# A chunked RWKV-7 recurrence with a GELU layer: the loads of v, b and k issued behind N and its blocks, and the sums of decays in four 64x64 tiles

## Chip, cores and metric

The kernel runs on one core of one Trainium2 chip. The metric is the device time of one execution in microseconds (us). The core has a tensor engine (PE; its weight loads are listed as PEld), a vector engine (VectorE, DVE), a scalar engine (ScalarE, ACT), GpSimd (POOL) and SyncE (SP), which here issues nearly all transfers; sixteen DMA engines carry these out. All engines run in parallel, each through its own instructions in a fixed order, and wait for each other by semaphores.

## What is computed

The first block is a recurrence over 768 steps for 4 batches of 8 heads with 40 channels. The state is a 40x40 matrix for each head. The second block is a dense layer with exact GELU.

```python
for t in range(S):                      # S = 768; r, k, v, w, a, b: [4, 8, 768, 40]
    y[:, :, t] = einsum('bhd,bhde->bhe', rt, state)
    Sa = einsum('bhde,bhe->bhd', state, at)
    state = state * wt[:, :, None, :] - einsum('bhd,bhe->bhde', Sa, bt)
    state = state + einsum('bhd,bhe->bhde', vt, kt)
x = y.transpose(0, 2, 1, 3).reshape(3072, 320)
h = x @ w_in                            # 320 x 2048
out = (0.5 * h * (1 + erf(h / sqrt(2)))) @ w_out    # 2048 x 320
```

Everything is 32-bit floating point.

## The kernel before

**Chunks.** The 768 steps are cut into 12 chunks of 64 steps. Within a chunk the recurrence becomes matrix products: running products of the decay w (`sums`: logarithms times a triangle of ones, then Exp), scaled copies of a, b and k, the masked products N = b·a, A = k·a, RV = v·r and M, and the inverse of (1 - N). The state goes from one chunk to the next. On 128 partitions lie two halves of 64: `half(e)`. Four batches are two pairs: batch `G*e + g` has e = 0 or 1 for the half of the partitions and g = 0 or 1 for a place in a row.

**The loop of a chunk's inverse.** `make_N(c)` (L100 for the products, L549 for the mask on VectorE) writes N to DRAM with four transfers (L586). `start_inverse` reads the 32x32 diagonal blocks back as Nb (L635), one block to a partition, and GpSimd inverts them column by column: 31 columns, each a product (L643) and an addition (L645) in W. `store_inverse` writes W to DRAM as inv from GpSimd's own queue (L657). In the next iteration SyncE fetches it as Tt and T (L667, L671), VectorE turns a part of it to L (L680), and TensorE makes J from L and N (`corner`), X from the state (`make_X`), and so on.

**The main loop** runs over c from 2 to 11 and works on three chunks at once: the recurrence of chunk c, the products A, av and RV of chunk c + 1, and loads, decay sums, N and the inverse of chunk c + 2 (n and n2 in the code). Between these it calls `fill()`, which takes one piece of the dense layer of an earlier chunk: 40 matrix products of ph and a GELU (L901, L903), or, from the fourth chunk on, one of four steps of `seven`, a Strassen-like scheme for the second product with seven instead of eight block products (L854; its sums on VectorE are L858, L868, L869, L875). The order of every engine is the order of the program text: nothing is rescheduled.

**SyncE's order in an iteration** follows from that: four stores of results, w, a, r, b and v and k for the turned copies, the moves of the recurrence's output xt into the layout of the dense layer (L802, L805), then v into VR (L200), rows of b and of k (L153), then Tt and T of chunk n (L667, L671), then N of chunk n2 (L586) and Nb (L635). An issue whose operands aren't ready holds up all that follow. Transfers take one of eight semaphores in turn, and an issue waits, where needed, for the transfer that had the same one, eight before it.

**Names.** `w_tile` holds w and then its logarithm. `pt` (wT_ps in the profile) holds the running sums turned, 64 steps along the row; `wp` (wpT) and `en` are their Exp with plus and minus. `cum` holds the same sums with steps on partitions; their negative Exp `rw` (part) scales the rows of b (L463, VectorE, result `nb` in b_rows) and of k (L470, GpSimd, result `ks` in k_rows). Both are used late, in `make_QY`. `extra` and `NB = 4` belong to the first four chunks, which load and turn differently.

Of the kernel before, what the change touches and what calls it, by code (L numbers as in the profile page):

```python
# [12 lines left out]
ALU = mybir.AluOpType  # L13
# [6 lines left out]
def kernel(  # L20
# [78 lines left out]
    def mm(o, lhsT, rhs, first=True):  # L99
        nc.tensor.matmul(o, lhsT, rhs, start=first, stop=True, skip_group_check=True)  # L100
# [48 lines left out]
    def fetch(c, n, src, eng, t=None):  # L149
        if t is None:  # L150
            t = rows({"b": b_rows, "k": k_rows}[n][0 if c < NB else c % 2])
        for e in range(2):
            eng.dma_start(out=t[half(e)].rearrange("p g h d -> p (g h) d")[:, :, :D], in_=rows_of(src, c, e))  # L153
        raws[c, n] = t
# [23 lines left out]

    def load_w(c, t=None, eng=nc.sync):
        t = w_tile if t is None else t  # L180
        fetch(c, "w", w, eng, t[:, :G * DM].rearrange("p (g h d) -> p g h d", g=G, h=H))
        raws[c, "w"] = t

    def by_64(t):
# [8 lines left out]
    def load_kb(c):  # L193
        fetch(c, "b", b, nc.sync)
        fetch(c, "k", k, nc.sync)

    def load_VR(c):
        VR = turned_in.setdefault(c, {})["VR"] = VR_ring()
        for e in range(2):
            nc.sync.dma_start(out=VR[half(e)].rearrange("p g q m d -> p (g q m) d")[:, :, :D], in_=rows_of(v, c, e))  # L200
# [206 lines left out]
    def sums(c):  # L407
        logw = raws.pop((c, "w"))
        pt = duo("wT_ps").rearrange("p e (n t) -> p e n t", t=C)
        for n in range(G * NP):  # L410
            for x in range(2):
                for e in range(2):
                    at = (2 * n + x) * D
                    mm(pt[half(x), e, n], logw[half(e), at:at + HP], cum_m[half(e), half(e)])
        cum = duo("cum")[:, :, :DM]
        for g in range(G):
            mm(cum[:, g], cum_m, logw[:, g * DM:(g + 1) * DM])
        wp = wp_ring()
        nc.scalar.activation(wp[:, :, 1:].rearrange("p (n e) t -> p e n t", e=2), pt, ACT.Exp)
        turned_in.setdefault(c, {})["wp"] = wp  # L420
        if c >= NB:
            en = turned_in.setdefault(c, {})["en"] = by_batch(side("en", "kT", 1))
            nc.scalar.activation(en.rearrange("p (e n) t -> p e n t", e=2), pt, ACT.Exp, scale=-1.0)
        rw = (avs_ring if c in (1, 2) else part_ring)()[:, :, :DM]
        nc.scalar.activation(rw, cum, ACT.Exp, scale=-1.0)
        decays[c] = rw.rearrange("p g (h d) -> p g h d", h=H), wp
# [37 lines left out]
        turned_in[c]["nb"] = nb  # L464

    def scale_k(c, eng=nc.gpsimd):
        rwv, _ = decays.pop(c)
        ks = turned_in[c]["ks"] = padded[:, 2 + c % 2] if c < NB else k_rows[c % 2]
        to = ks[:, :, :, :D] if c < NB else rows(ks)
        eng.tensor_tensor(to, raws.pop((c, "k")), rwv, ALU.mult)  # L470
# [226 lines left out]
    def joined(c):  # L697
        t = turned_in[c]
        Tt, T2 = inverses.pop(c)
        Js = t.pop("Js")  # L700
        F = flat(Tt)
        J = duo("J2")[:, :, :G * NP * BL].rearrange("p z (n t) -> p z n t", n=G * NP)
        for n in range(2 * G * NP):
            for q in range(2):
                if n % 2:
                    mm(J[lo[q], 1, n // 2], Js[lo[q], n // 2], T2[lo[q], n // 2])
                else:
                    mm(J[lo[q], 0, n // 2], Js[hi[q], n // 2], F[hi[q], n, BL:])
        for q, copy in ((0, nc.scalar.copy), (1, nc.vector.tensor_copy)):
            copy(F[lo[q], :, BL:].rearrange("p (n z) t -> p z n t", z=2), J[lo[q]])  # L710
        t["Tt"] = Tt
# [115 lines left out]
    def block(g, z):  # L827
        return gt[:, z * NF // 2:(z + 1) * NF // 2, g * P:(g + 1) * P]
# [15 lines left out]
    def seven(c, s1, s2):  # L844
        t1, t2, t4 = sums_of_w
        t3 = quarter(0, 1)
        os = [work.tile([P, 2, DM // 2], FP32, tag="os", name="os", bufs=2) for g in range(G)]
        c11, c12, c21, c22 = os[0][:, 0], os[0][:, 1], os[1][:, 0], os[1][:, 1]

        def products_of(*factors):  # L850
            po = duo("po")
            for n, (l_, r_) in enumerate(factors):
                for f in range(NF // 2):
                    nc.tensor.matmul(po[:, n, :DM // 2], l_[:, f], r_[:, f], start=f == 0, stop=f == NF // 2 - 1)  # L854
            return po[:, 0, :DM // 2], po[:, 1, :DM // 2]

        def add(to, one_, other):
            nc.vector.tensor_tensor(to, one_, other, ALU.add)  # L858

        def store(g):  # L860
            for e in range(2):
                row = (G * e + g) * S + c * C
                nc.sync.dma_start(out=out[row:row + C], in_=os[g][half(e)].rearrange("p z d -> p (z d)"))

        m1, m2 = products_of((block(0, 0), quarter(0, 0)), (block(0, 1), quarter(1, 0)))
        if s2 is None:
            s2 = SM_ring().rearrange("p e g n c -> p (e g n c)")[:, :NF * P // 2].rearrange("p (f t) -> p f t", t=P)
            nc.vector.tensor_tensor(s2, s1, block(0, 0), ALU.subtract)  # L868
        nc.vector.tensor_tensor(block(1, 0), block(0, 0), block(1, 0), ALU.subtract)  # L869
        nc.scalar.copy(c12, m1)  # L870
        nc.scalar.copy(c11, m2)
        add(c11, c11, c12)
        yield
        m5, m6 = products_of((s1, t1), (s2, t2))
        nc.vector.tensor_tensor(block(0, 1), block(0, 1), s2, ALU.subtract)  # L875
        nc.scalar.copy(c22, m5)  # L876
        add(c12, c12, m6)
        yield
        m3, m7 = products_of((block(0, 1), quarter(1, 1)), (block(1, 0), t3))
        add(c21, c12, m7)  # L880
        add(c12, c12, c22)
        add(c12, c12, m3)
        add(c22, c22, c21)
        store(0)
        yield
        m4, _ = products_of((block(1, 1), t4))
        add(c21, c21, m4)
        store(1)
        yield
# [231 lines left out]
    for c in range(2, NCH):  # L1121
        n, n2 = c + 1, c + 2
        more, more2 = n < NCH, n2 < NCH
        corner(c)
        make_X(c)
        if c == NS + 1:
            weight_sums(3)
        if c == 2:

            seconds(1, (14, 14), last=True)  # L1130
            fill()
            turn_b(n)
            make_N(n)
            run(start_inverse(n, nc.gpsimd))
            store_inverse(n, (nc.gpsimd,))
            load_r(n)
            load_v(n)
        else:
            fill()
        if more2:  # L1140
            load_next(n2)
        joined(c)
        if c == 2:
            pieces.reverse()
            seconds(2, last=True)
        fill()
        make_sa(c)
        make_saT(c)
        if c == 2:
            turn_r(n)  # L1150
            scale_k(n, nc.vector)
            fill()
            pieces.reverse()
            fill(2)
            turn_k(n)
        if more2:
            load_r(n2)
        if more2:
            turn_a(n2)
            fetch_pairs(n2, "b_turned", b, nc.sync, False, paired["a"])  # L1160
        fill()
        make_y2(c)
        make_M(c)
        if more:
            turn_v(n)
        if more2:
            load_v(n2)
            turn_r(n2)
            fetch_pairs(n2, "k_turned", k, nc.sync, False, paired["r"])
        fill()  # L1170
        if more2:
            logs(n2)
        make_QY(c)
        outputs(c)
        pieces.append(mlp(c))
        fill()
        if c == NS:
            weight_sums(0)
            weight_sums(1)
        if more:  # L1180
            make_A(n)
        if more2:
            load_VR(n2)
            load_kb(n2)
            sums(n2)
        if more:
            turn_state()
            fetch_inverse(n)
            make_av(n)
        if more2:  # L1190
            scale_a(n2)
            turn_b(n2)
        fill()
        if c == NS:
            weight_sums(2)
        if more:
            make_RV(n)
        if more2:
            make_N(n2)
            scale(n2)  # L1200
            run(start_inverse(n2, nc.gpsimd))
            store_inverse(n2, (nc.gpsimd,))
        if more:
            turn_corner(n)
        fill()
        if more2:
            turn_k(n2)
        fill()
# [31 lines left out]
```

## Time and profile before

| What | Value |
|---|---|
| Time, median of 3 runs (lowest, highest) | 731.21 us (728.41, 731.35) |
| Span of the profiled execution | 724.5 us |
| PE busy | 663.1 us (92%) |
| PEld busy | 582.5 us (80%) |
| DVE busy | 383.5 us (53%) |
| POOL busy | 352.8 us (49%) |
| ACT busy | 213.8 us (30%) |
| Mean rate of all transfers | 105 GB/s, 75.75 MB in all |
| GpSimd waits for Nb (10 times) | 104.9 us |
| GpSimd waits for k before L470 (8 times) | 64.9 us |
| SyncE waits for inv before Tt (4 times) | 23.7 us |

The table gives busy time and waits over the whole run. A long wait of an engine tells only that it has nothing to do; whether it costs anything depends on who waits for that engine next. So three views matter more here: the chain of waits that ended last, the timeline of each engine around one chunk, and busy time in stretches from one X to the next. In a timeline row the columns are the start, the length, the engine, the line, the operation and tiles, the count, and in brackets the idle time before it with what ended it.

### The profile page before, as it was taken

What the parts mean: (1) busy time and instruction counts of PE and PEld (TensorE: products, weight loads), DVE (VectorE), ACT (ScalarE), POOL (GpSimd) and SP (SyncE); (2) the same over time, 40 slices, a digit from 0 to 9 for tenths busy, and PEclk for the clock granted to TensorE, in tenths of its full rate; (3) what the DMA queues carried; (4) which work ended last, traced back from release to release, by engine and by line L of the source; (5) the groups of instructions that cost most, each with busy time, mean ns of one, the idle gap of its engine ahead of it and who ended that gap; (6) DMA issues with size and microseconds to landing.
All of it is one profiled execution on the core that took longest, in us unless ns stands there. A gap on an engine that the chain in (4) does not pass through costs nothing.

```text
span 724.5 us, 31335 instructions
## 1 busy us (share of the span) xinstructions
PE 663.1 (92%) x14096; PEld 582.5 (80%) x14096; DVE 383.5 (53%) x541; ACT 213.8 (30%) x279; POOL 352.8 (49%) x794
## 2 busy tenths in 40 slices
PE   6455889569999999999999999999999999999997
PEld 4345778557787887899899898998898998888987
DVE  2786569885255176275374473663762752621403
ACT  5114455343141240341341332222312413112020
POOL 4285248810761671862852853863854845810000
PEclk9655799779999999999999999999999999999999
DMA  7887739653766747657666666656566561020000
GB/s 118 135 168 145 138 93 216 132 109 80 132 129 99 144 85 137 108 99 137 109 115 126 113 113 125 116 95 132 111 102 125 104 106 50 22 53 3 25 14 19
DMA packets 284302, 75.75 MB, mean 105 GB/s; under 512 B 271976, under 2 KB 276872, under 8 KB 284168
## 3 DMA queue, kind: packets, MB, share of 16 engines
q1 hardware_dynamic: 283104, 71.22, 52.0%
q0 software_dynamic: 864, 2.36, 1.8%
q8 instruction: 111, 1.82, 1.1%
q14 instruction: 23, 0.19, 0.1%
q10 hardware_dynamic: 200, 0.16, 0.1%
HBM read 59.54 MB, written 10.22 MB: 96 GB/s over the span
## 4 chain that ended last, share of the span: by engine, by line
PE 49%; POOL 19%; DMA 10%; SPq 7%; DVE 7%; issue 5%; ACT 2%; ACTq 1%; DVEq 0%; POOLq 0%
PE ph L901 17%; POOL W L645 8%; POOL tmp L643 8%; PE po L918 8%; PE po L854 7%; PE QY L100 3%; DMA inv<-W 3%; DMA N<-N 3%; DMA Nb<-N 2%; PE cum L100 1%; PE J L100 1%; POOL st L643 1%; SPq L153 1%; POOL st L645 1%; PE X L100 1%
## 5 line engine op out<-in xcount | busy, mean ns | idle before, releaser
L901 PE MATMUL ph<-xt,w_in_sb 64*128 64x256 f32 x1920 | 221.1, 383 | 0.8 <-ACT gt L903 0.8
L901 PEld LDWEIGHTS ph<-xt,w_in_sb 64*128 64x128 f32 x1920 | 183.4, 188 | 23.9 <-ACT gt L903 0.5
L643 POOL TENSOR_TENSOR tmp<-W,Nb 128x126 f32<-128x126 f32 (+22 forms) x310 | 129.7, 418 | 128.4 <-DMA Nb<-N 104.9
L645 POOL TENSOR_TENSOR W<-W,tmp 128x126 f32<-128x126 f32 (+22 forms) x310 | 133.7, 431 | 24.3
L903 ACT ACTIVATE gt<-ph 128x1024 f32<-128x1024 f32 x48 | 49.1, 1023 | 148.6 <-PE ph L901 124.5
L854 PE MATMUL po<-w_out_sb,gt 128*128 128x160 f32 x576 | 82.9, 302 | 0.1
L854 PEld LDWEIGHTS po<-w_out_sb,gt 128*128 128x128 f32 x576 | 78.7, 190 | 2.2 <-DVE gt L875 0.4
L918 PE MATMUL po<-w_out_sb,gt 128*128 128x320 f32 x192 | 55.3, 444 | 0.0
L918 PEld LDWEIGHTS po<-w_out_sb,gt 128*128 128x128 f32 x192 | 36.6, 194 | 15.4 <-issue 1.1
L470 POOL TENSOR_TENSOR k_rows<-k_rows,part 128x640 f32<-128x640 f32 x8 | 12.3, 1542 | 64.9 <-DMA k_rows<-in_k_dram 64.9
L549 DVE TENSOR_TENSOR SM<-M_ps,upper 128x1024 f32<-128x1024 f32 x12 | 14.7, 1224 | 46.1 <-PE M_ps L100 46.1
L710 DVE COPY Tt<-J 32x512 f32<-32x512 f32 x12 | 8.3, 689 | 54.0 <-ACT Tt L710 54.0
L694 ACT COPY Js<-J 128x256 f32<-128x256 f32 x12 | 4.5, 371 | 101.6 <-PE J L100 101.6
L906 DVE TENSOR_TENSOR half<-gt 128x1024 f32<-128x1024 f32 x9 | 11.8, 1308 | 38.6 <-ACT gt L903 38.6
L303 ACT ACTIVATE conv<-conv,rebias 128x320 uint32<-128x320 uint32 (+1 forms) x26 | 16.1, 625 | 35.4 <-DVE conv L302 35.1
L854 PE MATMUL po<-extra,half 128*128 128x160 f32 x176 | 26.1, 303 | 0.0
L738 DVE COPY SM<-sap 128x640 f32<-128x640 f32 x12 | 9.9, 824 | 28.3 <-PE sap L100 28.2
L903 ACT ACT_TABLE_LOAD x10 | 12.8, 1283 | 40.0 <-PE ph L901 39.9
L854 PEld LDWEIGHTS po<-extra,half 128*128 128x128 f32 x176 | 24.2, 190 | 0.3
L858 DVE TENSOR_TENSOR os<-os,po 128x160 f32<-128x160 f32 x36 | 11.3, 315 | 24.8 <-ACT os L876 14.5
L549 DVE TENSOR_TENSOR VR<-RV_ps,upper 128x1024 f32<-128x1024 f32 x12 | 14.7, 1224 | 17.3 <-PE RV_ps L100 17.3
L680 DVE STREAM_TRANSPOSE L<-Tt 128x512 f32<-128x512 f32 x12 | 8.5, 711 | 27.4 <-DMA Tt<-inv 27.4
(197 smaller groups left out, 1130.6 us busy)
## 6 DMA issues: line engine op xcount, KB each, us to landing
Nb<-N SPq DMA_DIRECT2D x22, 256.0 KB
VR<-in_v_dram SPq DMA_DIRECT2D x24, 160.0 KB
out_dram<-os SPq DMA_DIRECT2D x48, 80.0 KB
w_tile<-in_w_dram SPq DMA_DIRECT2D x22, 160.0 KB
b_rows<-in_b_dram SPq DMA_DIRECT2D x22, 160.0 KB
k_rows<-in_k_dram SPq DMA_DIRECT2D x22, 160.0 KB
w_out_sb<-in_moe_w_out_dram SPq DMA_DIRECT2D x11, 320.0 KB
N<-N SPq DMA_DIRECT2D x48, 64.0 KB
```

The source lines that it names most:

```text
L100: nc.tensor.matmul(o, lhsT, rhs, start=first, stop=True, skip_group_check=True)
L303: nc.scalar.activation(power, power, ACT.Relu, bias=rebias, scale=8.0)
L470: eng.tensor_tensor(to, raws.pop((c, "k")), rwv, ALU.mult)
L549: nc.vector.tensor_tensor(to, pt, upper.unsqueeze(1).to_broadcast([P, 2 * G * NP, C]), ALU.mult)
L643: eng.tensor_tensor(t, W[:, :rows, j:j + 1].to_broadcast([P, rows, rest]), Nb[:, j:j + 1, j + 1:].to_broadcast([P, rows, rest]), ALU.mult)
L645: eng.tensor_tensor(W[:, :rows, j + 1:], W[:, :rows, j + 1:], t, ALU.add)
L854: nc.tensor.matmul(po[:, n, :DM // 2], l_[:, f], r_[:, f], start=f == 0, stop=f == NF // 2 - 1)
L858: nc.vector.tensor_tensor(to, one_, other, ALU.add)
L901: nc.tensor.matmul(ph[:, x, s], w_in_sb[half(x), kt, p * P:(p + 1) * P], xt[half(x), kt], start=kt == 0, stop=kt == NK - 1)
L903: nc.scalar.activation(gt[:, 4 * q:4 * q + 4].rearrange("p (x s) t -> p x s t", x=2), ph, ACT.Gelu)
L906: nc.vector.tensor_tensor(s1, block(1, 0), block(1, 1), ALU.add)
L918: nc.tensor.matmul(po[:, g], gt[:, f, g * P:(g + 1) * P], w_out_sb[:, f], start=f == 0, stop=f == NF - 1)
```

## The change

It has five parts, all for the chunks that the main loop prepares.

- The loads of b and k rows and of v (VR) move from ahead of Tt, T, N and Nb to behind them in SyncE's order, so that N and its blocks needn't wait for them.
- GpSimd's scaling of k moves from ahead of the inverse to after its eighth column (`BL // 4`), since k now comes later. `decays` keeps its entry, so that b can be scaled after k.
- VectorE's scaling of b moves into the next iteration, after `joined`.
- In `seven`, the subtraction that makes block(1,0) moves behind that of block(0,1).
- From the fifth chunk (`c >= NB`) w's pair g = 1 is loaded with its two batches in exchanged halves. Then the four sums of cum (two halves, two pairs) are four 64x64 products, one in each quadrant of the array, in place of two products of 128x128 with a triangle whose off-diagonal quarters are zero. As the turned sums come out with e exchanged for g = 1, the two Exps that read them are split into two each, with the order put right as they write.

```diff
     def load_w(c, t=None, eng=nc.sync):
         t = w_tile if t is None else t
-        fetch(c, "w", w, eng, t[:, :G * DM].rearrange("p (g h d) -> p g h d", g=G, h=H))
+        to = t[:, :G * DM].rearrange("p (g h d) -> p g h d", g=G, h=H)
+        if c < NB:
+            fetch(c, "w", w, eng, to)
+        else:
+            for e in range(2):
+                for g in range(G):
+                    eng.dma_start(out=to[half(e ^ g), g],
+                                  in_=w[G * e + g, :, c * C:(c + 1) * C].rearrange("h t d -> t h d"))
...
         for g in range(G):
-            mm(cum[:, g], cum_m, logw[:, g * DM:(g + 1) * DM])
+            for e in range(1 if c < NB else 2):
+                q = half(e ^ g) if c >= NB else slice(0, P)
+                mm(cum[half(e) if c >= NB else q, g], cum_m[q, q], logw[q, g * DM:(g + 1) * DM])
         wp = wp_ring()
-        nc.scalar.activation(wp[:, :, 1:].rearrange("p (n e) t -> p e n t", e=2), pt, ACT.Exp)
         turned_in.setdefault(c, {})["wp"] = wp
-        if c >= NB:
+        if c < NB:
+            nc.scalar.activation(wp[:, :, 1:].rearrange("p (n e) t -> p e n t", e=2), pt, ACT.Exp)
+        else:
             en = turned_in.setdefault(c, {})["en"] = by_batch(side("en", "kT", 1))
-            nc.scalar.activation(en.rearrange("p (e n) t -> p e n t", e=2), pt, ACT.Exp, scale=-1.0)
+            for to, scale_ in ((wp[:, :, 1:].rearrange("p (g n e) t -> p g e n t", g=G, e=2), 1.0),
+                               (en.rearrange("p (e g n) t -> p g e n t", e=2, g=G), -1.0)):
+                for g in range(G):
+                    nc.scalar.activation(to[:, g], pt[:, ::1 - 2 * g, g * NP:(g + 1) * NP], ACT.Exp, scale=scale_)
...
     def scale_k(c, eng=nc.gpsimd):
-        rwv, _ = decays.pop(c)
+        rwv, _ = decays[c]
...
-        nc.vector.tensor_tensor(block(1, 0), block(0, 0), block(1, 0), ALU.subtract)
         nc.scalar.copy(c12, m1)
         nc.scalar.copy(c11, m2)
         add(c11, c11, c12)
         yield
         m5, m6 = products_of((s1, t1), (s2, t2))
         nc.vector.tensor_tensor(block(0, 1), block(0, 1), s2, ALU.subtract)
+        nc.vector.tensor_tensor(block(1, 0), block(0, 0), block(1, 0), ALU.subtract)
...
         joined(c)
+        if c > 2 and more:
+            scale_b(n)
...
         if more2:
-            load_VR(n2)
-            load_kb(n2)
             sums(n2)
...
             make_N(n2)
-            scale(n2)
-            run(start_inverse(n2, nc.gpsimd))
+            steps = start_inverse(n2, nc.gpsimd)
+            load_kb(n2)
+            load_VR(n2)
+            for _ in range(BL // 4):
+                next(steps)
+            scale_k(n2)
+            run(steps)
             store_inverse(n2, (nc.gpsimd,))
```

## The prediction

> **What bounds the kernel now.** I read the page's chain of waits first. Its shares name two bounds, TensorE and a loop of GpSimd and DMA:
>
> ```profile
> PE 49%; POOL 19%; DMA 10%; SPq 7%; DVE 7%; issue 5%; ACT 2%; ACTq 1%; DVEq 0%; POOLq 0%
> ```
>
> The chain in order of time separates them. From 252 to 415 us it is TensorE alone. From 415 to 645 us it is one round repeated: N to DRAM, its blocks back (Nb), the inverse on GpSimd, the inverse to DRAM (inv), Tt back. Next, busy time chunk by chunk (stretch, length, then PE, PEld, DVE, ACT, POOL, granted clock, DMA share, GB/s):
>
> ```profile
> 338.20:388.90 50.70, 50.70 (x1184) 46.16 (x1180) 28.24 (x35) 15.41 (x20) 29.29 (x68) 1.00 0.65 117
> 439.70:491.30 51.60, 50.76 (x1182) 46.17 (x1182) 28.57 (x35) 15.40 (x20) 31.73 (x68) 1.00 0.60 114
> 491.30:543.10 51.80, 50.81 (x1184) 46.15 (x1180) 28.56 (x35) 15.41 (x20) 31.85 (x68) 1.00 0.62 116
> 543.10:596.50 53.40, 52.49 (x1190) 47.43 (x1182) 28.42 (x35) 15.41 (x20) 32.07 (x68) 0.97 0.60 112
> ```
>
> The first row has no idle TensorE: 50.7 us is its own price of a chunk. In the others it waits about 0.9 us each (the last also has a clock of 0.97). TensorE's timeline says for what:
>
> ```profile
> 489.51 0.74 PE L100 MATMUL J<-L,N 32*32 32x32 f32 x64 [0.84 <-DVE L L680]
> 541.37 0.74 PE L100 MATMUL J<-L,N 32*32 32x32 f32 x64 [0.98 <-DVE L L680]
> 594.75 0.74 PE L100 MATMUL J<-L,N 32*32 32x32 f32 x64 [0.91 <-DVE L L680]
> ```
>
> L is turned from Tt, so these are waits for the loop. Chunk 11 adds 0.65 us at J, chunk 10 0.96 at av. Together 4.3 us: all that a quicker loop alone can give. More must come out of the 50.7 us.
>
> SyncE's timeline shows why the loop is late (start, length, transfer):
>
> ```profile
> 424.98 1.41 SPq L200 DMA_DIRECT2D VR<-in_v_dram  x2
> 426.45 2.12 SPq L153 DMA_DIRECT2D b_rows<-in_b_dram  x2
> 428.61 3.58 SPq L153 DMA_DIRECT2D k_rows<-in_k_dram  x2
> 432.62 3.18 SPq L667 DMA_DIRECT2D Tt<-inv  x4
> 435.85 0.99 SPq L671 DMA_DIRECT2D T<-inv  x2
> 436.94 2.02 SPq L586 DMA_DIRECT2D N<-N  x4
> ```
>
> VectorE had N masked at 432.7, yet N is issued at 436.9, behind the rows. In the five rounds from 225 us on, issue minus mask is 4.5, 2.3, 1.8, 2.5 and 4.2 us. After that SyncE waits for inv itself, and the loop runs on its own length: 51.8 us from Tt at 486.20 to Tt at 537.98.
>
> **What the skill says.** The Trainium skill, SBUF — State Buffer, "Who interferes with whom": a DVE instruction with two SBUF inputs contends with a GpSimd instruction that reads SBUF, and the later one blocks. The trace agrees: the inverse's 56-element add takes 0.30 us at 502.36, but 1.22 at 528.69, inside nT times en on VectorE (528.52 to 529.75). The skill's TensorEngine Tiling, "Tiling Modes": 64x64 gives four independent tiles. It agrees: one 64x104 matmul instruction of QY lasts 249 ns, 128 of them take 3.01 us, 23.5 ns each. The skill's DMA: Bandwidth & Descriptors, "Queues, rings and completion order": a ring's descriptors are consumed in order, so rows behind Nb should not overtake it; the trace of before has no such order to show it.
>
> **The change, part by part.**
>
> *Rows of v, b, k behind N and Nb.* Their six issues take 5.1 us (476.39 to 482.31) to 7.2 us. In the SyncE-bound rounds N now goes when masked, 1.8 to 4.5 us earlier. In the round after 415 us: mask at 432.7 less 2.8 (the tiles below, five chunks) is 429.9; Tt and T in front of N cost 3.05 us after inv has landed (486.20 to 489.24), which gives about 431 instead of 436.9, a lead of 6 us. Further, inv travels without the rows: with rows beside it 6.3, 5.0 and 6.4 us from issue to Tt, without them (635.59 to 640.78) 5.2; I take 5.2, a gain of about 0.7 a round.
>
> *k scaled after eight columns.* The 1.54 us of L470 used to lie in GpSimd's wait for Nb (11.0 us at 499.99) and cost nothing. Now it lies inside the inverse: +1.54 us a round. Should k be late, GpSimd waits with 23 columns queued behind: k's issue ends about 4 us after Nb's, rows land some 4 us after that (482.31 to 486.62), and Nb plus eight columns needs 5 + 6 us (499.99 to 506.1). It arrives first, by about 3 us: no wait.
>
> *b scaled after joined.* 0.82 us on VectorE, put before SM, where it waits 2.76 us for sap: hidden for TensorE. But it has two SBUF inputs and now falls in the inverse: 0 to 0.8 us, I take 0.5.
>
> *block(1,0) later.* 1.42 us on VectorE (521.76) leaves the stretch ahead of A's mask and runs after L875, ahead of the second half of a product pair whose first half takes 2.3 us of TensorE: hidden. If the inverse has ended by then (4 us of lead suffice), one block of GpSimd, about 0.9 us, goes.
>
> *Four 64x64 tiles for cum.* Before: four instructions of 128x320, 1.18 us from cum's start to the next (319.93 to 321.11). Four tiles need eight instructions of about 0.27 us; side by side as QY's are (3.7 times) 0.58 us plus a start, so 0.63; one after another more than 1.18. I take the first: 0.55 us saved in each of eight chunks, 4.4 us, on the path wherever TensorE is the bound. It is the only edit that lowers the 50.7.
>
> *Exps in halves.* wp and en, 1.03 and 1.02 us, become four of 512 elements; that size costs 0.59 alone and starts every 0.49 in a pair (saT at 503.24 and 503.72). +0.1 us on ScalarE before en is done; po takes that buffer about 0.5 us later. No cost. w's four issues for two: at most 0.5 us of SyncE.
>
> *What the rows delay.* Out, w and a now queue behind six issues. Also the program lets each issue wait for the DMA eight before it, which today holds a back until Nb has landed (issue at 500.19, Nb at 499.99); after, out waits so. I put a 7 us later. VectorE turns a at 506.42, 16.2 us after X; 7 us later it would push M's mask, which QY awaits at X + 24.0, by 1.6 us. This bites only where X follows Tt's issue by 4.1 us, as now; with 6 us or more between them it vanishes. It limits itself, so I cost it at 0.5 us in all.
>
> **The sum.** A round is 3.05 (Tt, T) + 10.1 (N issue to first column, 489.24 or 384.51 on) + inverse + 5.2. The inverse took 30.2 to 31.3 us while X came 6 to 10 us after Tt's issue, and 33 when it came 4 us after, since then more of VectorE's two-input work falls into it. With the lead restored: 31.3 + 1.54 + 0.5 - 0.9 = 32.4, and the round is 50.8 against TensorE's new 50.15. From N at 431 three rounds and the last inverse end at 431 + 3 x 50.8 + 10.1 + 32.4 + 5.2 = 631.1. The last X needs that plus 4.1, 635.2; TensorE alone brings it to 644.9 - 4.3 - 4.4 = 636.2. So the loop is just hidden: 8.7 us, less 0.5, leaves 731.2 - 8.2 = 723 us.
>
> **Rivals.** *The loop still binds the end.* For: the reserve is 1 us over four rounds, and scaled k is pure addition. With a round of 52.3 the last inverse lands at 637.2 and X at 641.3: 3.6 us gained, 728. *The tiles don't run side by side:* only the waits go, 4.3 us, 727. Against: QY's 23.5 ns. *The loop gets longer than it was.* Rows behind Nb slow it by 0.7, the inverse stays at 33 and pays 1.54 + 0.8: 54.4 a round, last inverse at 645.4, X at 649.5, 4.6 us later than now: 736. For: the blocks seen on GpSimd and the late a, which keeps VectorE's work inside the inverse. Against: inv's freer path, and a lead of 6 us at the start.
>
> **Chances.** Forecast 723: 0.53, with some of it down to 719, where the rounds shrink and nothing else is lost. Loop still binds, 728: 0.22. Tiles serial, 727: 0.10. Longer loop, 736: 0.15. The bound of 0.5% is 3.7 us, 727.5: faster gets 0.53, half of the two middle cases (0.16), 0.69 in all; same 0.16; slower 0.15. The range for eight in ten: 718 to 732.
>
> **What would show it.** Right: cum at about 0.6 us a chunk; N issued within 0.5 us of its mask until about 430 us; J waits gone or under 0.3 us; PE's rows at 50.1 without idle; the inverse about 32.5 us with k's scaling inside and no wait before it. Wrong: waits at J as now; GpSimd idle before k's scaling; the inverse at 35 us; VectorE waiting for a and TensorE for M's mask at QY; SyncE reaching Tt after inv has landed.

## The result and the profile after

| | Median, us | Ratio to before (95% interval) |
|---|---|---|
| Before, 4 runs | 730.09 | |
| Changed kernel, 4 runs | 718.38 | 0.9853 (0.9807 to 0.9900) |
| Changed kernel again, 22 runs, beside 55 of before (median 730.16) | 723.41 | 0.9895 (0.9866 to 0.9925) |

The change is a gain. Its size is better read from the second row: 1.05%, or 7.7 us. Medians are over all runs; the ratios leave out runs more than 1.5% above the fastest of their kernel, among them the one that was profiled in the second measurement. For the second measurement 721 to 723 us were expected from the two profiles, and 718 to 719 if the first measurement's 11.7 us were all the change's; 723.4 came.

Times scatter by some 10 us from run to run. Part of this lies at the start: the third X, which ends the part with the weight conversions, starts at 232 to 234 us in some profiles and at 237 to 240 in others. The granted clock differs there: 0.86 between 60 and 120 us in the changed kernel's profile (third X at 232.5), 0.79 in that of e6 (238.0). So kernels are compared below by time and by the stretch from the third X to the last. This stretch fell from 411.4 us (233.5 to 644.9) to 403.4 (232.5 to 635.9), 8.0 us.

The stretch scatters too. The second measurement's profile of the changed kernel, e5, is of an execution of 728.6 us. Its stretch is 407.4 us (239.4 to 646.8), only 4.0 us shorter than before's, and its last J waits long for the loop:

```profile
646.10 0.74 PE L100 MATMUL J<-L,N 32*32 32x32 f32 x64 [2.07 <-DVE L L693]
```

TensorE is idle for 5.1 us of the stretch, against 2.0 in the first profile; its busy time is nearly the same, 402.3 and 401.4 us, and its clock 1.00 in both. A difference of up to 4 us between the stretches of two kernels therefore proves little by itself. What follows in this section is from the first profile.

In the chain, GpSimd's share falls from 19% to 16%, and the others move by at most a point. Busy time chunk by chunk in the changed kernel (columns as before: length, then PE, PEld, DVE, ACT, POOL, clock, DMA share, GB/s):

```profile
335.50:385.60 50.10, 50.10 (x1190) 45.51 (x1184) 29.20 (x35) 15.53 (x22) 29.00 (x68) 1.00 0.64 114
385.60:435.70 50.10, 50.10 (x1194) 45.52 (x1184) 28.52 (x35) 15.53 (x22) 28.80 (x68) 1.00 0.65 119
435.70:486.60 50.90, 50.42 (x1196) 45.68 (x1184) 28.43 (x35) 15.53 (x22) 28.97 (x68) 1.00 0.66 119
486.60:537.10 50.50, 50.35 (x1187) 45.61 (x1184) 28.68 (x35) 15.53 (x22) 29.88 (x68) 1.00 0.64 117
```

TensorE's price of a chunk is now 50.1 us. Idle time is left in two of these rows (0.5 and 0.15 us). SyncE's timeline of the round that was shown for before:

```profile
426.74 2.10 SPq L680 DMA_DIRECT2D Tt<-inv  x4
428.88 1.96 SPq L684 DMA_DIRECT2D T<-inv  x2
430.94 2.04 SPq L599 DMA_DIRECT2D N<-N  x4
434.50 1.14 SPq L648 DMA_DIRECT2D Nb<-N  x2
435.73 1.37 SPq L153 DMA_DIRECT2D b_rows<-in_b_dram  x2
437.15 3.61 SPq L153 DMA_DIRECT2D k_rows<-in_k_dram  x2
440.80 1.57 SPq L207 DMA_DIRECT2D VR<-in_v_dram  x2
```

N goes at 430.9 where it went at 436.9, with the mask done at 429.9. In the four rounds before this one it goes within 0.1 us of its mask. TensorE's timeline around cum (tn_ps, the turned state, comes next), before and then after:

```profile
318.87 1.13 PE L100 MATMUL wT_ps<-cum_m,w_tile 64*64 64x64 f32 x64
319.93 1.34 PE L100 MATMUL cum<-w_tile,cum_m 128*128 128x320 f32 x4
321.11 1.04 PE L433 MATMUL tn_ps<-ident,st 128*128 128x128 f32 x8
```

```profile
317.84 1.11 PE L100 MATMUL wT_ps<-cum_m,w_tile 64*64 64x64 f32 x64
318.77 0.72 PE L100 MATMUL cum<-w_tile,cum_m 64*64 64x320 f32 x8
319.42 1.09 PE L446 MATMUL tn_ps<-ident,st 128*128 128x128 f32 x8
```

From the same engine's timeline, its waits in the first two rounds and the last (av is the product of VR and A):

```profile
215.42 1.14 PE L100 MATMUL av<-VR,A 64*64 64x40 f32 x64 [0.61 <-ACT en L436]
268.26 1.14 PE L100 MATMUL av<-VR,A 64*64 64x40 f32 x64 [0.45 <-ACT en L436]
621.23 1.14 PE L100 MATMUL av<-VR,A 64*64 64x40 f32 x64 [0.32 <-DVE A L562]
635.26 0.74 PE L100 MATMUL J<-L,N 32*32 32x32 f32 x64 [0.54 <-DVE L L693]
```

From wT_ps to tn_ps takes 1.58 us where it took 2.24. The wait for en is new, and the wait of the last J is what remains of the four.

In the whole stretch TensorE's idle time fell from 4.3 to 2.0 us and its busy time from 407.0 to 401.4. Of the 5.6 us of busy time 1.7 are before's chunk with a clock of 0.97, in which TensorE ran at half clock for some 3.4 us, right behind the wait of 0.98 us at J (541.37):

```profile
544.00:546.00 2.00, 2.00 (x14) 1.60 (x12) 1.77 (x3) 0.00 (x0) 0.00 (x0) 0.50 0.10 12
```

Other profiles have such stretches too; the last section counts them. The other 3.9 us are TensorE's lower price of a chunk, over seven chunks.

### The profile page after: what moved, and what is told of

The parts are those of the page before. It is cut to its first block, busy times and chain, and to the rows that moved or that the text cites. A ratio compares the mean times of both kernels' runs of the same rounds, so it can differ in the third digit from the quotient of the medians.

```text
span 716.1 us, 31454 instructions
## 1 busy us (share of the span) xinstructions
PE 656.9 (92%) x14128; PEld 575.5 (80%) x14128; DVE 383.7 (54%) x541; ACT 214.6 (30%) x295; POOL 343.6 (48%) x794
## 4 chain that ended last, share of the span: by engine, by line
PE 49%; POOL 16%; DMA 11%; DVE 8%; SPq 7%; issue 5%; ACT 3%; ACTq 1%; POOLq 0%; DVEq 0%
PE ph L914 18%; PE po L931 8%; POOL W L658 8%; PE po L867 8%; POOL tmp L656 7%; PE QY L100 3%; DMA inv<-W 3%; DMA Nb<-N 2%; DMA N<-N 2%; PE J L100 2%; SPq L153 1%; DMA Tt<-inv 1%; DMA w_out_sb<-in_moe_w_in_dram 1%; DVE conv L314 1%; PE av L100 1%
## 5 line engine op out<-in xcount | busy, mean ns | idle before, releaser
L656 POOL TENSOR_TENSOR tmp<-W,Nb 128x126 f32<-128x126 f32 (+22 forms) x310 | 125.0, 403 | 164.4 <-DMA Nb<-N 141.5
L658 POOL TENSOR_TENSOR W<-W,tmp 128x126 f32<-128x126 f32 (+22 forms) x310 | 129.4, 418 | 24.3
L176 DVE STREAM_TRANSPOSE aT<-a_pairs 128x1024 f32<-128x1024 f32 x9 | 11.2, 1245 | 43.2 <-DMA a_pairs<-in_a_dram 43.2
L100 PE MATMUL av<-VR,A 64*64 64x40 f32 x768 | 15.7, 240 | 9.0 <-DVE A L562 7.3
L100 PEld LDWEIGHTS av<-VR,A 64*64 64x64 f32 x768 | 14.0, 149 | 11.3 <-DVE A L562 7.9
```

The source lines that it names most:

```text
L176: nc.vector.transpose(to.rearrange("p n (s y) -> p n y s", y=2), raws.pop((c, n)).rearrange("p n (y d) -> p n y d", y=2)[:, :, :, :BL])
L656: eng.tensor_tensor(t, W[:, :rows, j:j + 1].to_broadcast([P, rows, rest]), Nb[:, j:j + 1, j + 1:].to_broadcast([P, rows, rest]), ALU.mult)
L658: eng.tensor_tensor(W[:, :rows, j + 1:], W[:, :rows, j + 1:], t, ALU.add)
```

## The experiments

Each has a share of the change undone or done alone. In the table, the inverse is the mean time of the last four from their first column to the issue of inv. The first profile of the changed kernel stands for it; in its second, e5, the stretch is 407.4 us and the inverse 33.1.

| Kernel | Median, us | Ratio (95% interval) | Third X to last, us | Inverse, us |
|---|---|---|---|---|
| before | 730.16 | | 411.4 | 32.6 |
| changed | 723.41 | 0.9895 (0.9866 to 0.9925) | 403.4 | 32.6 |
| e1: tiles alone | 729.82 | 0.9995 (0.9968 to 1.0021) | 413.5 | 31.8 |
| e11: tiles, block | 725.41 | 0.9943 (0.9915 to 0.9971) | 409.6 | 31.6 |
| e2: rows alone | 725.95 | 0.9934 (0.9911 to 0.9957) | 406.9 | 33.3 |
| e10: rows, block | 722.31 | 0.9896 (0.9850 to 0.9943) | 406.4 | 32.0 |
| e3, e7: rows, tiles | 726.66, 725.76 | 0.9952, 0.9956 | 407.1, 407.9 | 33.8, 33.7 |
| e4, e6: changed, k on VectorE | 723.09, 722.57 | 0.9872, 0.9892 | 403.9, 402.8 | 31.4, 31.2 |
| e9: as e6, block first | 722.44 | 0.9893 (0.9840 to 0.9947) | 403.7 | 32.3 |
| e12: as e6, no tiles | 724.12 | 0.9926 (0.9900 to 0.9953) | 406.1 | 30.6 |
| e8: rows between T and N | 773.78 | 1.0579 (1.0509 to 1.0648) | 448.4 | 34.0 |

("Rows" includes k after eight columns and b after joined; "block" is block(1,0)'s move.)

**e1: tiles alone.** The kernel before with `load_w` and `sums` of the change, nothing else.

```diff
-            mm(cum[:, g], cum_m, logw[:, g * DM:(g + 1) * DM])
+            for e in range(1 if c < NB else 2):
+                q = half(e ^ g) if c >= NB else slice(0, P)
+                mm(cum[half(e) if c >= NB else q, g], cum_m[q, q], logw[q, g * DM:(g + 1) * DM])
```

> The kernel before with one part of the change: w's exchanged halves, cum in four 64x64 tiles, Exps in halves. Theory (two bounds that need each other): TensorE's price of a chunk falls by 0.6 us, from 50.7 to 50.1, but the rows still stand ahead of N, so the loop of GpSimd and DMA keeps its length of about 52 us and binds earlier. Expected: waits at J of 1.2 to 1.8 us in the last three or four rounds where there were 0.9, and a gain of only 2 to 3 us of the 4.8 that the tiles are worth; span 721.5 to 722.5. Rival (the loop was never the bound, its waits were slack): the full 4.8 us, span below 720.

No gain at all: 0.9995. TensorE's timeline still has the waits at J, one of them at 1.53 us:

```profile
391.62 0.74 PE L100 MATMUL J<-L,N 32*32 32x32 f32 x64 [0.91 <-DVE L L693]
497.83 0.74 PE L100 MATMUL J<-L,N 32*32 32x32 f32 x64 [1.53 <-DVE L L693]
```

The first comes two chunks earlier than any such wait did before. And SyncE still holds N: its mask was done at 440.7.

```profile
435.10 2.10 SPq L207 DMA_DIRECT2D VR<-in_v_dram  x2
437.25 1.69 SPq L153 DMA_DIRECT2D b_rows<-in_b_dram  x2
438.98 3.07 SPq L153 DMA_DIRECT2D k_rows<-in_k_dram  x2
442.16 2.25 SPq L680 DMA_DIRECT2D Tt<-inv  x4
444.45 0.98 SPq L684 DMA_DIRECT2D T<-inv  x2
445.53 2.04 SPq L599 DMA_DIRECT2D N<-N  x4
```

But the waits at J did not grow as the theory has it. They are 0.91, 1.53, 0.20 and 0.38 us, 3.0 in all against 3.4 before. What ate the tiles' saving in this profile is something else: half clock, which costs 5.1 us of TensorE in two chunks (clocks of 0.97 and 0.94) against 1.7 before, and 2.15 us at X in which it waits for nothing that shows. All of this stands behind the two waits above. So the saving is lost while the loop is late, but only one profile says on what; the time says only that it is lost.

**e2: rows alone.** The kernel before with the moves of the loads and of both scalings.

```diff
             make_N(n2)
-            scale(n2)
-            run(start_inverse(n2, nc.gpsimd))
+            steps = start_inverse(n2, nc.gpsimd)
+            load_kb(n2)
+            load_VR(n2)
+            for _ in range(BL // 4):
+                next(steps)
+            scale_k(n2)
+            run(steps)
```

> The kernel before with the other part alone: rows of v, b, k behind N and Nb, k scaled after eight columns, b after joined; cum stays in two 128x320 products, block(1,0) stays first. Theory: the waits at J go, TensorE's price stays at 50.7; a gain of 3.5 to 4.3 us, span 720.2 to 721. Rival (the inverse is longer by 1.5 us of k and sets the end): J waits as before or longer, span 724 or more.

4.1 us less by the medians (730.03 beside it), 4.5 in the stretch (406.9), of which about 1.3 are before's chunk with a clock of 0.97 (52.49 us busy, 51.23 here). Chunks take 50.7 us, and the three J waits from 489 us on are gone; left are 0.76 us at av and 0.47 at the last J. The theory's mechanism and size hold; the span it named (720.2 to 721) was missed, 725.1, as the third X fell at 238.6.

**e3 and e7: rows and tiles without block(1,0)'s move,** measured twice, the second time (e7) beside the changed kernel.

```diff
+        nc.vector.tensor_tensor(block(1, 0), block(0, 0), block(1, 0), ALU.subtract)
         nc.scalar.copy(c12, m1)
...
         nc.vector.tensor_tensor(block(0, 1), block(0, 1), s2, ALU.subtract)
-        nc.vector.tensor_tensor(block(1, 0), block(0, 0), block(1, 0), ALU.subtract)
```

> The changed kernel with block(1,0) back ahead of A's mask. Theory: the 1.4 us on VectorE have room there and the loop has a reserve, so within 0.6 us of the changed kernel (span 715.7 to 716.7), the inverse up to 0.9 us longer. Rival (A's mask comes late and av waits for it, since a and so VectorE's work is later now): 0.5 to 1 us in each of seven chunks, span 719 to 722.

> The changed kernel with block(1,0) back ahead of A's mask, again, beside the changed kernel. Its first profile had inverses about 1 us longer and J waiting 0.9 and 1.7 us in the last two rounds. Theory revised by that (the reserve of the loop is under 1 us a round, so 1 us more of VectorE's two-input work inside the inverse brings the waits back): 2 to 4 us more than the changed kernel. Rival (my first: hidden): within 0.6 us of it.

The first theory fell: beside the changed kernel the median of e7 is 2.4 us higher, and the ratios are 0.9952 (0.9925 to 0.9978) and 0.9956 (0.9924 to 0.9989) against 0.9895 (0.9866 to 0.9925), so that the intervals just touch. Both inverses are about 1.1 us longer than in the changed kernel's first profile (0.6 or 0.7 than in e5), and TensorE waits again (e7):

```profile
595.13 0.74 PE L100 MATMUL J<-L,N 32*32 32x32 f32 x64 [0.89 <-DVE L L693]
631.98 1.14 PE L100 MATMUL av<-VR,A 64*64 64x40 f32 x64 [0.80 <-DVE A L562]
645.75 0.74 PE L100 MATMUL J<-L,N 32*32 32x32 f32 x64 [0.28 <-DVE L L693]
```

So the loop's reserve in the changed kernel is smaller than 1 us a round. The stretches don't add to this: e5, the changed kernel itself, has 407.4 us and waits at J of 0.32 and 2.07. It is the times that speak for block(1,0)'s move.

**e4 and e6: k scaled on VectorE,** one kernel, measured twice.

```diff
         if c > 2 and more:
             scale_b(n)
+            scale_k(n, nc.vector)
...
-            for _ in range(BL // 4):
-                next(steps)
-            scale_k(n2)
             run(steps)
```

> The changed kernel with k scaled by VectorE right after b, after joined, and no longer by GpSimd inside the inverse. Theory (the loop is just hidden): the inverse falls by 0.7 to 1.5 us a round, but only the remaining waits of TensorE (0.5 us at the last J and a few tenths) can go: 0.3 to 1.3 us less than the changed kernel, span 714.8 to 715.8. Rival (the loop still sets the end through the last four rounds): 0.7 to 1.5 us a round, 3 to 6 us less, span 710 to 713. Third possibility: SM waits behind b and k on VectorE (0.8 and 0.9 us against 1.9 us of idle) and nothing is gained.

> The kernel with k scaled on VectorE, again, now beside the changed kernel. Its first profile had no wait at J at all and inverses of 30.4 to 32.5 us against 31.4 to 33.6. Theory (the loop is just hidden in the changed kernel): 0.3 to 1.3 us less than the changed kernel in the same call, from the last J (0.5 us) and what stands before it. Rival (the loop still sets the end): 3 us or more less.

The inverse falls by 1.2 to 1.4 us and no J waits at all, yet the time stays: ratio 0.9872 (0.9822 to 0.9922) and 0.9892 (0.9860 to 0.9924) against 0.9895, medians of e6 and the changed kernel 0.8 us apart, stretches of 403.9 and 402.8 against 403.4. That speaks against the rival, which has 3 us or more, but the ratios are uncertain by 0.3% (2 us) and more. In the changed kernel's first profile the loop is just hidden; in e5 (407.4) it is not quite. No gain in time from scaling k on VectorE is shown.

**e9: k on VectorE, block(1,0) first.** The edit of e6 with that of e3.

> Rows behind N, tiles, and k scaled on VectorE, but block(1,0) ahead of A's mask. So far: rows alone 0.9934 of before, rows and tiles without block(1,0)'s move 0.9952 and 0.9956, all of it 0.9895. Theory (the tiles pay only where the loop has a reserve, and any 1 us taken from the inverse gives it): k on VectorE takes the place of block(1,0)'s move, inverses of 31 to 33 us, no J wait over 0.5 us, ratio 0.988 to 0.991. Rival (block(1,0)'s move helps by TensorE's waits for A's mask, not by the loop): ratio stays at 0.994 to 0.996, and av waits.

Inverses of 32.2 to 32.4 us, no J wait, stretch 403.7, though av still waits 0.79 us for A's mask, once. The trace speaks for the theory: with another microsecond taken from the inverse, the loop is hidden although block(1,0) stands first, which suggests that its move gives the changed kernel room in the loop. With six runs the ratio's interval, up to 0.9947, doesn't exclude the rival.

**e10: rows and block, no tiles.** e2 with block(1,0) moved.

> Rows behind N and block(1,0) moved, but cum in two 128x320 products. Theory: rows alone already have no J wait until the last round, so a longer reserve gives nothing but that one's 0.5 us: ratio 0.992 to 0.9945, TensorE's chunk at 50.7 us. Rival (block(1,0)'s move is worth 2 to 3 us by itself): 0.990 or less.

Inconclusive in time: 0.9896, an interval of nearly a per cent with six runs, which holds both answers. The trace speaks for the theory: no J wait, chunks of 50.7 us, a stretch 0.5 us shorter than e2's, 3 us longer than the changed kernel's in its first profile (1 us shorter than in e5). In time this kernel without tiles is level with the changed one (0.9896 and 0.9895), so no gain from the tiles shows here.

**e11: tiles and block, rows ahead of N.** e1 with block(1,0) moved.

> Tiles and block(1,0) moved, but the rows still ahead of Tt and N. Theory (SyncE's order makes the loop late; tiles alone were 0.9995): the inverse gets up to 1 us shorter, N still stands behind the rows, J keeps waits of 0.3 to 1.5 us in the last rounds: ratio 0.995 to 0.999. Rival (a shorter inverse is all that the tiles lacked): 0.992 or less.

0.9943 lies just outside the theory's range, and its interval (0.9915 to 0.9971) reaches into both. J waits 0.58 and 2.12 us in two rounds, and behind the longer wait come 1.62 us at X without a visible cause and 6.8 us of half clock. The last four inverses are only 0.2 us shorter than e1's, all eight of the main loop 0.7 (30.8 against 31.5). N still stands behind the rows, 2.3 to 7.1 us after its mask, and the ratio lies between those of e1 and the changed kernel: that fits a shorter inverse giving part of the gain and SyncE's order withholding the rest, but doesn't prove it.

**e12: no tiles where the loop is hidden.** The kernel of e6 with `load_w` and `sums` of before.

> Rows behind N, block(1,0) moved and k scaled on VectorE, but cum in two 128x320 products: the kernel with k on VectorE (723 us, ratio 0.987 to 0.989) less its tiles. There J never waited, so here TensorE alone is the bound and the tiles can be priced. Theory (the tiles are worth 0.6 us a chunk wherever the loop is hidden): chunks of 50.7 us without J waits, 407 us from the third X to the last where the tiles gave 403 to 404, ratio 0.992 to 0.995. Rival (what the tiles save on TensorE is lost to other waits of theirs, such as for the halved Exps and for issue before av): within 1 us of the tiled kernel from the third X to the last, ratio 0.988 to 0.9905.

Two chunks of e12, then two of e6, neither with a wait at J:

```profile
392.30:443.10 50.80, 50.80 (x1194) 46.26 (x1184) 29.24 (x36) 15.41 (x20) 28.06 (x67) 1.00 0.64 114
443.10:493.80 50.70, 50.70 (x1184) 46.19 (x1184) 28.98 (x36) 15.40 (x20) 27.93 (x67) 1.00 0.66 121
```

```profile
391.50:441.70 50.20, 50.20 (x1190) 45.59 (x1187) 29.23 (x36) 15.54 (x22) 27.80 (x67) 1.00 0.65 118
441.70:492.10 50.40, 50.36 (x1191) 45.64 (x1188) 29.39 (x36) 15.53 (x22) 28.11 (x67) 1.00 0.64 119
```

The stretch is 406.1 us against 403.9 and 402.8 (e4, e6): by these profiles the tiles are worth 2.2 to 3.3 us, not the 4.2 that seven chunks of 0.6 make. That is within the 4 us by which two profiles of the changed kernel differ; TensorE's busy time, which waits don't touch, agrees with 405.5 us against 402.1 and 401.7. The ratios (0.9926, 0.9892) stand as the theory has them, but their intervals overlap. Part of the rival is true: the first chunk of the stretch gains nothing, for av waits 0.51 us for en in e6; and waits of 0.2 to 0.3 us without a visible cause ("issue") appear near av.

**e8: rows between T and N.** The changed kernel with the six row loads put after `fetch_inverse` and ahead of N.

```diff
             fetch_inverse(n)
+            if more2:
+                load_kb(n2)
+                load_VR(n2)
             make_av(n)
...
             steps = start_inverse(n2, nc.gpsimd)
-            load_kb(n2)
-            load_VR(n2)
```

> The changed kernel with one thing moved: the rows of b, k and v are issued after Tt and T but ahead of N, no longer behind Nb. inv and Tt travel without them as in the changed kernel. Theory (N's place in SyncE's order is what counts): N goes 5 to 7 us later after Tt, each round is that much longer than the loop's 51 us, and TensorE waits 3 to 6 us at J in the last four or five rounds: 15 to 25 us more than the changed kernel, slower than the kernel before too. Rival (what counted was the rows' traffic beside inv): within 1.5 us of the changed kernel.

```profile
450.52 1.92 SPq L680 DMA_DIRECT2D Tt<-inv  x4
452.49 0.98 SPq L684 DMA_DIRECT2D T<-inv  x2
453.56 1.43 SPq L153 DMA_DIRECT2D b_rows<-in_b_dram  x2
455.08 2.71 SPq L153 DMA_DIRECT2D k_rows<-in_k_dram  x2
457.84 1.49 SPq L207 DMA_DIRECT2D VR<-in_v_dram  x2
459.42 2.54 SPq L599 DMA_DIRECT2D N<-N  x4
```

The theory's cause holds, but it put the size at about half. N goes 8.9 us after Tt in place of 4, though its mask was done at 445.07, 14 us before; the inverse is 1.4 us longer; and a round takes 57 us. J waits 1.9 us at the end of the second round of the stretch and 3.6 to 5.1 us in each of the six after it, 28 us in all, so the loop binds earlier than expected. From the third chunk on TensorE's clock is 0.93 to 0.95 in each, with half clock around every wait at J: its busy time is 418.8 us, 17 more than in the changed kernel. Together the stretch is 45 us longer. The rows' traffic is the same and inv has the same free path; only N's place differs. It is the order in SyncE's queue that counts.

## Why the prediction was right

The forecast was 723 us, 8.2 less. Measured are 718.4 with few runs and 723.4 with many, a gain of 7.7 us by the ratio.

- **Two bounds, 4.3 us of waits:** right in kind. In the first profile TensorE's idle time falls from 4.3 to 2.0 us. That the waits were all that a quicker loop alone can give was too little: 1.7 us of half clock behind one of them went as well (e2, the quicker loop alone, gained 4.5 us in the stretch although it kept 1.4 us of idle time). In e5 the idle time is 5.1 us, 2.4 of it in the last round, and the stretch gains 4.0 us: that is close to the rival *The loop still binds the end* (3.6).
- **N goes when masked:** right, 430.94 against the 431 named. Within 0.1 us in four rounds, then 0.6 to 2.5 us later, when SyncE waits for inv.
- **A round, 50.8 us:** the three from N at 430.94 to N at 583.85 take 51.0 on average, by terms that were off both ways. From Tt to N it is 4.0 us where 3.05 was put, from inv to Tt 5.6 where 5.2 was put (the free path of inv gives 0.3 us a round, not 0.7), from N to the first column 9.2 where 10.1 was put. The errors nearly cancel.
- **Rows behind Nb:** they cost nothing that shows. From N's issue to the first column takes 9.0 us (mean of the last four; 9.5 in e5, 10.3 before). The order alone didn't promise this: the Trainium skill's DMA: Bandwidth & Descriptors, "Queues, rings and completion order", also says that a later descriptor may finish its write before an earlier one. The six issues that were read as 5.1 us (476.39 to 482.31) are 5.9; no sum used them.
- **k after eight columns, no wait before it:** right. It starts with no idle time in any round and takes 1.54 us there.
- **b after joined:** right for TensorE. It takes 0.82 to 1.57 us, and VectorE's next operation, the copy of sap into SM, still waits 1.2 to 1.9 us for TensorE in the four chunks from 344 to 496.
- **The inverse, 32.4 us:** 32.6 (33.1 in e5). Last inverse landed at 631.1 by the sum; Tt was issued at 631.2. Last X forecast 636.2; it came at 635.9. But the third X was 1.0 us earlier than before's, from which the sum starts: the stretch is 403.4 us where 402.7 was forecast, and 407.4 in e5.
- **block(1,0):** its 0.9 us of GpSimd are 1.1 (e3, e7; 0.6 or 0.7 beside e5). It was counted in the sum, but not seen to be necessary: e3's first expectation called it hidden. The chance of 0.22 for a loop that still binds names the state that e7 is in, and the end of e5.
- **Tiles, 0.55 us a chunk:** 0.60 in a chunk that isn't disturbed. In eight chunks 4.4 us were put; over seven, e12 gives 2.2 to 3.3 by its profile. A step that failed is *Exps in halves, no cost*: in the first two rounds TensorE waits 0.61 and 0.45 us for en, which takes most of what the tiles save there. The halves themselves added only the 0.1 us that was put: in the first of these rounds en ends 3.25 us after wT_ps starts, and 3.13 before. What was overlooked: in the kernel before, en was done at 215.91 and av started at 215.98, so a TensorE that gets to av some 0.65 us sooner has to wait. From the third round on av starts before en is done.
- **The rows delay a:** overestimated. VectorE turns a 20.3 us after X (455.99, X at 435.74), 4.1 us later than in the same round before, not 7 (3.0 to 6.3 over seven rounds), and M's mask follows without a gap:

```profile
455.99 1.25 DVE L176 STREAM_TRANSPOSE aT<-a_pairs 128x1024 f32<-128x1024 f32 x1 [7.42 <-DMA a_pairs<-in_a_dram]
457.16 1.18 DVE L562 TENSOR_TENSOR SM<-M_ps,upper 128x1024 f32<-128x1024 f32 x1
```

M's mask ends at 458.3, QY needs it at X + 24, 459.7: 1.4 us to spare.

- **Rivals:** tiles one after another is out (eight instructions from 318.77 to the next at 319.42), and so is a longer loop (51.0 us a round, 51.8 before). A loop that still binds the end is not out: e5 shows it.

The sum of the last X came out to 0.3 us with two terms of a round off by 0.9 us in opposite directions and a third X that was 1.0 us early; so much agreement is partly luck. Not settled: what the waits for issue come from, which stand mostly in kernels with tiles; how often the changed kernel ends as e5 does; and whether the tiles' 2 to 3 us can be shown in the time, which scatters by more.

## What to carry to other kernels

Where a loop over DMA and a second engine runs beside the engine that is full, price both per round and keep the difference in mind: here 50.1 us against about 51, with a lead that the early rounds save up. An edit that lowers one alone is worth nothing beyond that difference (tiles alone 0.9995), and a small edit elsewhere, such as one operation of 1.2 us moved out of the inverse's time, can decide whether another pays (0.9956 without that move, 0.9895 with it). In a queue with a fixed order, put the short transfers that a loop waits for ahead of bulk rows that are needed much later; the same rows a few places earlier cost 45 us. And compare two profiles of one kernel before a difference between two kernels is read from one profile of each: here the same stretch of the same kernel was 403.4 and 407.4 us.

## What the runs showed of the hardware

Three things were not expected. Four 64x320 products on the four quadrants (eight instructions) take 0.65 us to the next operation where two of 128x320 took 1.18, and a chunk gains 0.60, not only the 0.53 between these: the 64x64 products of wT_ps ahead of them give way 0.13 us earlier too (0.93 us from wT_ps to cum, 1.06 before).

A wait of TensorE can cost more than its length. From the third X on, the granted clock falls to 0.50 in thirteen places in these profiles (one in before, two in e1, one each in e3, e7 and e11, seven in e8), each time during a wait of 0.89 us or more at J or within 5 us after it. The half clock lasts about 3.4 or 6.8 us, and so takes up to 1.7 or 3.4 us of TensorE's time. It doesn't follow every such wait: of seventeen J waits of 0.84 us or more, four have none behind them (0.84, 0.87, 0.91 and the 2.07 of e5). The seven profiles without a J wait over 0.55 us have no half clock in this stretch. Which waits bring it and why stays open.

The first 230 us differ by 5 to 6 us between profiles of the same kernel (third X at 232.6 in e3, 238.5 in e7), with granted clocks of 0.86 and 0.79 between 60 and 120 us: more than most of the edits here are worth.
